# Scan and top-1 expert kernel: traced landing times in the build-time scheduler, six chunks turned by TensorE, new ranks

## The chip, the core and the metric

The kernel runs on one core of one Trainium2 chip. The metric is the device time of one execution in microseconds (us); a figure for a kernel is the median of several executions. A profiled execution gives the trace, from which all the rows below are read. TensorE is PE in the profile, VectorE DVE, ScalarE ACT, GpSimd POOL and SyncE SP.

## What is computed

Two steps, one behind the other, over 4 sequences of 5056 tokens with 256 channels each. The first is a gated recurrence along the sequence; the second sends each token to one of 8 experts (256 to 1024 to 256).

```python
sig = 1.0 / (1.0 + np.exp(-f_logit))
f = lower_bound + (1.0 - lower_bound) * sig
h[t] = f[t] * h[t - 1] + (1 - f[t]) * x[t]          # per sequence and channel, h starts at 0

logits = h @ w_gate
e_idx = np.argmax(logits, axis=1)
gate_w = softmax(logits)[e_idx]
eom = sigmoid(h @ w_output_gate)
out[token] = gate_w * eom[e_idx] * (relu(h @ w1[e_idx]) @ w2[e_idx])
```

## The kernel before

**Chunks.** The 20224 tokens are worked on in 40 chunks of up to 512. For each chunk SP's queue loads two halves of 512 KB each, `f` and `x` (L493, into one of four buffers, the tiles `fx`). ScalarE takes a tanh (L554) and the forget gate (L562), VectorE a product (L557) and the scan (L568), one of each for both halves of the channels. ScalarE squares (L577), TensorE sums the squares (L582), and from that VectorE takes a power of two for each channel (the small steps L341 to L351) by which the rows are split into a high part (ScalarE, L596) and a rest (VectorE, L599). TensorE then multiplies both by the gates (L629, L636). A chain of small steps on VectorE finds the expert of each token (L664 to L685) and its place in the expert's list (L692 to L738, `dst`); L748 to L756 write the two factors beside the row.

**Turning and scattering.** The rows leave the chunk token by token, so they are turned first. For chunks from `FLIP` on, SP's queue does it with four transposing DMAs a chunk (`turn`, L606, 128 KB each). For chunks ahead of `FLIP`, TensorE transposes (`flip`, L616, two times 8 matmuls of 128x128) and ScalarE copies the result to `rows` (`settle`, L622, two a chunk). GpSimd then scatters the rows to `scr` in device memory, 128 tokens an instruction (`send`, L760, four a chunk). Chunks 0, 6 and 8 are worked on together with the next one; so chunks 0 and 1 share one chain of small steps, and 2 has its own. Ahead of the first scatter two DMAs write the pad rows of `scr` (L451).

**Weights.** Each expert's weights come in four loads of 512 KB (L961, tiles `w1s`, `w2s` and a `spare`). TensorE sums their squares (L1002), VectorE finds a norm (L1011 and small steps, up to `cinv`, L1018), ScalarE writes the high part (L1025) and VectorE the rest (L1029).

**Expert tiles.** A tile is up to 256 tokens of one expert. SP's queue gathers its rows from `scr`, transposed (`xq`, L1068), with the factors (`mt`, L1071); a list (`firsts`, L876, read on SP by L1064) says where they lie. The first tile of each expert is made by `first` (L1174 to L1243): four quarters of 12 matmuls up (L1190 to L1192), a high part (ScalarE, L1197), a rest (VectorE, L1201, `el`) and 12 matmuls down (L1214 to L1216). The first tile of expert 0 needs chunks 0 to 2 scattered. The tiles after those are the same with their weights copied to a buffer (L1095 on VectorE; up L1120 to L1122, high part L1129, rest L1137, down L1168 to L1170). The result is scaled on ScalarE (L1254) and scattered to the output by GpSimd (L1258).

**What sets the order.** A scheduler runs when the kernel is built. Every operation is an `Op` with an engine, an estimated cost, the operations that it needs, and, for a DMA, `ship`, its share of the DMA rings. `Clock.start` estimates when an operation could start; `Clock.drive` takes, on each engine, those that could start within 0.2 us of the earliest, and of them the one with the lowest number in `RANK`; `Clock.run` emits it and books its end. So the tables of numbers and the estimates set the order in which each engine's instructions stand. Loads of chunks and of weights are held behind the VectorE instruction that was emitted last.

Of the kernel before, what the change touches and what calls it, by code (L numbers as in the profile page):

```python
# [43 lines left out]
AHEAD = 10  # L44
EIGHT = 6
RANK = {
    "setup": (-1.79,),
    "pad": (111.84,),
    "steady": (1083.0, -252.28, -120.37, -372.54, 593.86, 324.22, 400.43, 793.4,),
    "tiles": (686.39, 292.5, 1654.95, 552.0, 347.5, 547.63, 517.82,),  # L50
    "first": (-278.52, 1564.55,),
    "plan": (417.78, 434.95,),
    "load": (-665.55, -89.61, 940.76, 394.74, -259.08, 259.99, 78.44, 300.77, 561.91, 301.96,),
# [7 lines left out]
    "gram": (93.14, -61.7, 1485.49, -210.01, 145.26, 421.5, 1186.44, -100.15,),  # L61
    "norm": (436.94, -280.81, 498.9, -288.2, 719.44, -78.73, 333.59, 983.81,),
    "w0": (1378.71, -304.56, 873.38, -252.27, 459.78, -57.06, 397.41, 465.44,),
    "w1": (1021.41, 4435.66, 1660.07, -256.31, 878.52, -188.54, 427.66, 629.66,),
}
# [5 lines left out]
VEC, ACT, TEN, GPS, SYN = "VATGS"  # L71
# [3 lines left out]
BACKLOG = 2.0  # L75
FLIP = 3
QUICK = 10
# [10 lines left out]
class Op:  # L88


    def __init__(self, eng, cost, fn, needs=(), key=None, stage=0, ring=None, ship=0.0, bulk=False, lazy=False, group=None,
                 shift=0.0, lag=0.0, margin=0.0, late=False, gap=False):
        self.eng, self.cost, self.fn, self.needs, self.key = eng, cost, fn, tuple(needs), key
        self.group, self.shift = group, shift
        self.stage, self.ring, self.ship, self.bulk, self.lazy = stage, ring, ship, bulk, lazy
        self.lag, self.margin, self.late, self.gap = lag, margin, late, gap
        self.done = False
# [22 lines left out]
class Clock:  # L120
# [56 lines left out]
    def run(self, o, t):  # L177
# [15 lines left out]
        if o.ship:  # L193
            self.bus = max(self.bus, t + (1.2 if o.eng == GPS else min(o.cost, 1.0))) + o.ship
            end = self.bus + SHIP + (1.2 if o.bulk else 0.2)
            if o.eng == SYN:
                self.out.append(end)
        elif o.eng == TEN:
            end += 0.16
            if self.on and o.lag:  # L200
                end += o.lag
                self.aside.add(o.key)
# [33 lines left out]
def tile_scan_moe(  # L236
# [258 lines left out]
    def chunk_load(c):  # L495
        past = 0 if c < 4 else 4 if c < 6 else 2
        held = [("turned", c - past), (c - past, "pr"), (c - past + 1, "scan0"), (c - past + 1, "scan1")] if past else []
        group, shift = (("load", c), 0.0) if c < AHEAD else (("steady", 6), 2 * TILE * (c - AHEAD))
        return [
            Op(SYN, 0.5, lambda i=i: load_part(c, i), held, ("fx"[i], c), ship=1.34, bulk=True, group=group, shift=shift)  # L500
            for i in range(2)
        ]

    def bunch(i):
# [289 lines left out]
        for c in cs:  # L794
            for k in range(KD):
                op(7, ACT, 0.72, lambda c=c, k=k: high(c, k), ["sa", (c, "sq0"), (c, "sq1")], (c, f"h{k}"), c)
            for k in range(KD):
                op(8, VEC, 0.76, lambda c=c, k=k: rest(c, k), [(c, f"h{k}")], (c, f"l{k}"), c)
                if c >= FLIP:
                    op(8, SYN, 1.28, lambda c=c, k=k: turn(c, 0, k), [(c, f"h{k}"), *gone(c)], (c, f"turn0{k}"), c, ship=0.78)  # L800
            if c < FLIP:
# [6 lines left out]
            else:  # L808
                for k in range(KD):
                    turn1.append((10, SYN, 1.28, lambda c=c, k=k: turn(c, 1, k), [(c, f"l{k}"), *gone(c), *(["oh"] if c >= AHEAD else [])],  # L810
                                  ("turned", c) if k == KD - 1 else (c, f"turn1{k}"), c))
                    if c < AHEAD:
                        op(*turn1[-1], ship=0.78)
        prs = [(c, "pr") for c in cs]
# [9 lines left out]
        if c1 >= AHEAD:  # L824
            for x in turn1:
                op(*x, ship=0.78, late=True)
        op(14, TEN, 0.16 * (nb + 1) / 5, all_before, ["oh"], "pk", lag=1.4)
# [12 lines left out]
        for c in cs:  # L840
            for b in range(size[c] // P):
# [3 lines left out]
                   (c, "sent") if b == size[c] // P - 1 else None, c, ship=0.55, late=AHEAD <= c < NCH - 1 and b > 0,  # L845
                   gap=AHEAD <= c < NCH - 1)
        if c1 == NCH - 1:
# [110 lines left out]
    def expert_load(e):  # L958

        return [  # L960
            Op(SYN, 0.5, lambda h=h, z=z: nc.sync.dma_start(out=crude(e, h, z), in_=wT[SLOTS[e]][:, h * WH + z * QH : h * WH + (z + 1) * QH]),  # L961
               [(0, "sent")] if e == E - 1 else [], ("w", e, h, z), ship=1.32, bulk=True, group=("wl", e))
            for h in range(2) for z in range(2)
# [210 lines left out]
    def first(e):  # L1174
# [55 lines left out]
        need = [(c, "sent") for c in range(EARLY[e])] + [("tab", groups.index(EARLY[e])), ("free",)]  # L1230
        op(4 * e, SYN, 2.3, fetch, need, key("x"), ring=("xq", 3, key("up", 3)), ship=1.8)
        for q in range(4):
# [308 lines left out]
```

## Time and profile before

| | us |
|---|---|
| median of 3 runs | 955.34 |
| lowest, highest | 954.16, 959.31 |
| profiled execution | 959.21 |
| its span in the trace | 957.5 |
| TensorE busy | 903.9 (94%) |
| VectorE busy | 739.0 (77%) |
| ScalarE busy | 541.2 (57%) |
| GpSimd busy | 354.1 (37%) |

The span runs from the first to the last instruction in the trace; the execution's own time is 1.7 us longer. A busy share is a mean over the whole span, and this kernel has two parts: a front in which chunks and weights are made ready and no expert tile can run, and a long stretch in which TensorE has tiles throughout. So the profile has to be read by stretches. The mean granted clock of TensorE over the span was 0.98 of full speed.

### The profile page before, as it was taken

How to read it: one execution, taken by the hardware profiler on the slowest of the kernel's cores; microseconds unless marked ns; L12 is line 12 of the kernel's file. 1: busy time of each engine (PE TensorE's matmuls, PEld its weight loads, DVE VectorE, ACT ScalarE, POOL GpSimd, SP SyncE). 2: the span in 40 equal slices, each digit the busy share in tenths (PEclk: the TensorE clock that was granted, in tenths of full speed). 3: DMA queues.
4: the chain of work that ended last, by engine and by line, in shares of the span. 5: the costliest groups of instructions: out<-in, count | busy, mean ns of one | idle time of the engine just before them, and what ended most of it. 6: DMA issues, size and time to landing. Idle time of an engine off the chain costs nothing.

```text
span 957.5 us, 26500 instructions
## 1 busy us (share of the span) xinstructions
PE 903.9 (94%) x9504; PEld 812.7 (85%) x9504; DVE 739.0 (77%) x2048; ACT 541.2 (57%) x1184; POOL 354.1 (37%) x382
## 2 busy tenths in 40 slices
PE   3569999999999999999999999999999999999997
PEld 3458888888888888888888888888888888899996
DVE  6879889788877887878878789787888778445554
ACT  6959586656465655657556576464655543223332
POOL 1533163443534344343443435435344342212122
PEclk9669999999999999999999999999999999999999
DMA  9988974765656767666766658645666443112110
GB/s 334 350 187 225 290 202 95 201 158 135 152 148 180 148 157 153 145 175 155 169 146 139 184 146 169 151 131 149 166 166 155 109 114 92 51 34 61 42 44 26
DMA packets 229739, 144.44 MB, mean 151 GB/s; under 512 B 193611, under 2 KB 195404, under 8 KB 229600
## 3 DMA queue, kind: packets, MB, share of 16 engines
q1 hardware_dynamic: 214016, 99.90, 44.5%
q0 software_dynamic: 15296, 42.73, 13.6%
q8 instruction: 79, 1.29, 0.6%
q14 instruction: 60, 0.49, 0.2%
q10 hardware_dynamic: 288, 0.02, 0.0%
HBM read 58.38 MB, written 44.37 MB: 107 GB/s over the span
## 4 chain that ended last, share of the span: by engine, by line
PE 66%; DMA 10%; DVE 9%; issue 8%; ACT 4%; POOL 1%; SPq 0%; POOLq 0%; DVEq 0%; ACTq 0%
PE ph L1120 11%; PE py L1168 11%; PE ph L1121 10%; PE ph L1122 10%; PE py L1169 10%; PE py L1170 10%; DMA out_dram<-yo,mt 3%; DVE fx L568 3%; DMA fx<-in_xT_dram 3%; POOL out_dram L1258 1%; DMA fx<-in_fT_dram 1%; DVE fx L557 1%; DMA mt<-scr 1%; PE rw L636 1%; DVE el L1201 1%
## 5 line engine op out<-in xcount | busy, mean ns | idle before, releaser
L1122 PE MATMUL ph<-xq,w 128*128 128x256 f16 (+2 forms) x1312 | 326.6, 259 | 0.0
L1120 PE MATMUL ph<-xq,w 128*128 128x256 f16 (+2 forms) x1312 | 326.1, 259 | 0.3 <-DMA xq<-scr 0.3
L1121 PE MATMUL ph<-xq,w 128*128 128x256 f16 (+2 forms) x1312 | 326.4, 259 | 0.0
L1129 ACT ACTIVATE hh<-ph 128x512 f16<-128x512 f32 (+1 forms) x312 | 173.1, 555 | 246.0 <-PE ph L1122 218.6
L1168 PE MATMUL py<-w2s,hh 128*128 x1136 | 309.0, 272 | 2.5 <-issue 1.9
L1170 PE MATMUL py<-w2s,hl 128*128 x1136 | 309.4, 272 | 0.0
L1169 PE MATMUL py<-w2s,hh 128*128 x1136 | 309.2, 272 | 0.0
L1258 POOL DMA_INDIRECT out_dram<-yo,mt x146 | 157.3, 1078 | 291.5 <-ACT yo L1254 239.3
L760 POOL DMA_INDIRECT scr<-rows,dst x158 | 165.3, 1046 | 261.1 <-DVE hl L1137 34.5
L1137 DVE SCALAR_TENSOR_TENSOR hl<-ph,hh 128x512 f16<-128x512 f32 (+1 forms) x312 | 197.5, 638 | 68.1 <-ACT hh L1129 62.9
L1095 DVE COPY w<-w1s 128x2048 f16 x164 | 118.3, 721 | 43.4 <-PE ph L1122 36.7
L1120 PEld LDWEIGHTS <-w 128*128 128x128 f16 x1312 | 127.6, 98 | 12.0 <-issue 0.6
L1122 PEld LDWEIGHTS <-w 128*128 128x128 f16 x1312 | 127.4, 97 | 11.8
L1121 PEld LDWEIGHTS <-w 128*128 128x128 f16 x1312 | 127.4, 97 | 10.1
L1168 PEld LDWEIGHTS <-hh 128*128 128x128 f16 x1136 | 110.7, 97 | 15.2 <-issue 3.7
L1170 PEld LDWEIGHTS <-hl 128*128 128x128 f16 x1136 | 110.6, 97 | 13.1
L1169 PEld LDWEIGHTS <-hh 128*128 128x128 f16 x1136 | 110.6, 97 | 10.2
L568 DVE TENSOR_TENSOR_SCAN fx<-fx,fx 128x512 f32<-128x512 f32 (+4 forms) x78 | 95.0, 1238 | 3.4 <-ACT fx L562 3.3
L562 ACT ACTIVATE fx<-fx,fb,fa 128x512 f32<-128x512 f32 (+1 forms) x80 | 61.6, 801 | 33.8 <-DVE fx L557 33.8
L1254 ACT ACTIVATE yo<-py,fac 128x256 f32<-128x256 f32 (+1 forms) x146 | 61.9, 469 | 28.3 <-PE py L1170 24.1
L599 DVE SCALAR_TENSOR_TENSOR fx<-fx,sa 128x512 f16<-128x512 f32 (+1 forms) x80 | 55.9, 740 | 10.4 <-ACT fx L596 10.3
L636 PEld LDWEIGHTS <-fx 128*128 128x128 f16 x632 | 52.9, 97 | 7.4 <-DVE fx L599 1.5
(177 smaller groups left out, 1196.6 us busy)
## 6 DMA issues: line engine op xcount, KB each, us to landing
fx<-in_fT_dram SPq DMA_DIRECT2D x39, 512.0 KB
fx<-in_xT_dram SPq DMA_DIRECT2D x39, 512.0 KB
w1s<-in_wT_dram SPq DMA_DIRECT2D x14, 512.0 KB
w2s<-in_wT_dram SPq DMA_DIRECT2D x14, 512.0 KB
scr<-rows,dst POOLq DMA_INDIRECT x158
rows<-fx SPq DMA_TRANSPOSE x148
out_dram<-yo,mt POOLq DMA_INDIRECT x146
spare<-in_wT_dram SPq DMA_DIRECT2D x4, 512.0 KB
```

The lines of the kernel that those rows point to most:

```text
L568: nc.vector.tensor_tensor_scan(out=xt(c)[:, k, a:z], data0=ft(c)[:, k, a:z], data1=xt(c)[:, k, a:z], initial=init, op0=ALU.mult, op1=ALU.add,)
L760: ins = nc.gpsimd.indirect_dma_start(out=scr[:, :], out_offset=IOA(ap=H["dst"][:, j : j + 1], axis=0), in_=lines[:, j, :], in_offset=None)
L1095: nc.vector.tensor_copy(out=w, in_=w1f[:, ds(T["ev"] * (2 * WH) + h * 2 * QH, 2 * QH)])
L1120: nc.tensor.matmul(out=o, lhsT=w[:, f, k, 0, :], rhs=T["xh"][:, k, 0:n], start=first, stop=False)
L1121: nc.tensor.matmul(out=o, lhsT=w[:, f, k, 0, :], rhs=T["xl"][:, k, 0:n], start=False, stop=False)
L1122: nc.tensor.matmul(out=o, lhsT=w[:, f, k, 1, :], rhs=T["xh"][:, k, 0:n], start=False, stop=last)
L1129: nc.scalar.activation(hh[:, :, 0:n], ph[:, :, 0:n], AF.Relu)
L1137: nc.vector.scalar_tensor_tensor(out=hl[:, :, 0:n], in0=ph[:, :, 0:n], scalar=0.0, in1=hh[:, :, 0:n], op0=ALU.max, op1=ALU.subtract)
L1168: nc.tensor.matmul(out=o, lhsT=hh[:, i, c], rhs=wh, start=first, stop=False, skip_group_check=True)
L1169: nc.tensor.matmul(out=o, lhsT=hh[:, i, c], rhs=wl, start=False, stop=False, skip_group_check=True)
L1170: nc.tensor.matmul(out=o, lhsT=hl[:, i, c], rhs=wh, start=False, stop=last, skip_group_check=True)
L1258: ins = nc.gpsimd.indirect_dma_start(out=out[:, :], out_offset=IOA(ap=T["mt"][0 : T["p"], b, 2:4].bitcast(I32), axis=0), in_=T["yo"][0 : T ...
```

## The change

Four things change. `FLIP` goes from 3 to 6: the rows of chunks 3, 4 and 5 are turned by TensorE and copied by ScalarE, where SP's queue turned them with twelve transposing DMAs. The estimates of the scheduler change: a chunk's load, a weight's load and a transposing DMA take larger shares of the rings, and an operation can have a landing time (`land`), 2.0 for scatters and for the gathers of the first tiles, which is added to its end. All the ranks of the front are new numbers (two rows of the table stand below), and the rows "steady" and "tiles" of the table stay. Nothing else is changed; TensorE has 48 transposes more and ScalarE six copies more.

```diff
 RANK = {
...
     "steady": (1083.0, -252.28, -120.37, -372.54, 593.86, 324.22, 400.43, 793.4,),
     "tiles": (686.39, 292.5, 1654.95, 552.0, 347.5, 547.63, 517.82,),
-    "first": (-278.52, 1564.55,),
+    "first": (283.02, 978.35,),
...
-FLIP = 3
+FLIP = 6
...
-        self.lag, self.margin, self.late, self.gap = lag, margin, late, gap
+        self.lag, self.margin, self.late, self.gap, self.land = lag, margin, late, gap, land
...
-            end = self.bus + SHIP + (1.2 if o.bulk else 0.2)
+            end = self.bus + SHIP + (1.2 if o.bulk else 0.2) + o.land
...
-            Op(SYN, 0.5, lambda i=i: load_part(c, i), held, ("fx"[i], c), ship=1.34, bulk=True, group=group, shift=shift)
+            Op(SYN, 0.5, lambda i=i: load_part(c, i), held, ("fx"[i], c), ship=1.47, bulk=True, group=group, shift=shift)
...
-                    op(8, SYN, 1.28, lambda c=c, k=k: turn(c, 0, k), [(c, f"h{k}"), *gone(c)], (c, f"turn0{k}"), c, ship=0.78)
+                    op(8, SYN, 1.28, lambda c=c, k=k: turn(c, 0, k), [(c, f"h{k}"), *gone(c)], (c, f"turn0{k}"), c, ship=1.01)
...
-                   gap=AHEAD <= c < NCH - 1)
+                   gap=AHEAD <= c < NCH - 1, land=2.0)
...
-               [(0, "sent")] if e == E - 1 else [], ("w", e, h, z), ship=1.32, bulk=True, group=("wl", e))
+               [(0, "sent")] if e == E - 1 else [], ("w", e, h, z), ship=1.45, bulk=True, group=("wl", e))
...
-        op(4 * e, SYN, 2.3, fetch, need, key("x"), ring=("xq", 3, key("up", 3)), ship=1.8)
+        op(4 * e, SYN, 2.3, fetch, need, key("x"), ring=("xq", 3, key("up", 3)), ship=1.8, land=2.0)
```

How the instructions move is seen in each engine's order. In it `fx_135` is the buffer of chunk 0 and again of chunk 4, `fx_136` of 1 and 5, `fx_133` of 2, and `fx_134` of 3.

On SP, the loads behind chunk 0's stand like this before:

```order
L493 DMA fx_136<-in_fT_dram 128x2x512
L451 DMA scr<-padt 128x544 x2
L493 DMA fx_136<-in_xT_dram 128x2x512
L493 DMA fx_134<-in_fT_dram 128x2x512
L493 DMA fx_134<-in_xT_dram 128x2x512
L961 DMA w1s<-in_wT_dram 128x1024 x2
L961 DMA w2s<-in_wT_dram 128x1024 x2
L493 DMA fx_133<-in_fT_dram 128x2x512
L493 DMA fx_133<-in_xT_dram 128x2x512
```

And on SP in the changed kernel:

```order
L451 DMA scr<-padt 128x544 x2
L493 DMA fx_136<-in_fT_dram 128x2x512
L493 DMA fx_136<-in_xT_dram 128x2x512
L493 DMA fx_133<-in_fT_dram 128x2x512
L493 DMA fx_133<-in_xT_dram 128x2x512
L961 DMA w1s<-in_wT_dram 128x1024 x2
L961 DMA w2s<-in_wT_dram 128x1024 x2
L961 DMA w1s<-in_wT_dram 128x1024 x2
L961 DMA w2s<-in_wT_dram 128x1024 x2
L493 DMA fx_134<-in_fT_dram 128x2x512
```

Chunks 2 and 3 changed places, four weight loads instead of two stand ahead of the later of them, and the pad went ahead of chunk 1.

On SP, the end of the front, up to the first gather (`xq`), stands like this before:

```order
L961 DMA w2s<-in_wT_dram 128x1024 x2
L961 DMA w1s<-in_wT_dram 128x1024 x2
L961 DMA w2s<-in_wT_dram 128x1024 x2
L606 DMA_TRANSPOSE rows<-fx_134 128x4x128 x4
L961 DMA w1s<-in_wT_dram 128x1024
L1064 TENSOR_LOAD firsts
L1064 ISA x2
L1068 ISA
L1068 DMA_TRANSPOSE xq<-scr 128x4x256
```

And in the changed kernel:

```order
L961 DMA w1s<-in_wT_dram 128x1024 x2
L961 DMA w2s<-in_wT_dram 128x1024 x2
L961 DMA w1s<-in_wT_dram 128x1024 x2
L961 DMA w2s<-in_wT_dram 128x1024 x2
L1064 TENSOR_LOAD firsts
L1064 ISA x2
L1068 ISA
L1068 DMA_TRANSPOSE xq<-scr 128x4x256
```

The transposes of chunk 3 and the weight load that stood between them and the gather are gone from there.

On VectorE, around the first rest of an expert tile (`el`; `pf_n`, `done` are steps of the list `firsts`, `w1s` and `w2s` rests of weights, `es`, `eg` and `fc` factors of a chunk), before:

```order
L867 TENSOR_SCALAR pf_n<-pf_n 128x5
L869 TENSOR_SCALAR done_142<-pf_n 128x5
L871 TENSOR_TENSOR pf_n<-bfree,pf_n 128x5
L1029 SCALAR_TENSOR_TENSOR w1s<-w1s,wi 128x8x128 x2
L1201 SCALAR_TENSOR_TENSOR el<-ph,eh 128x512
L748 SCALAR_TENSOR_TENSOR fc<-es,eg 128x4
L1201 SCALAR_TENSOR_TENSOR el<-ph,eh 128x512 x2
```

And in the changed kernel (`cinv` ends the norms of a group of experts; `xr`, `xi` are powers of two of a chunk):

```order
L1018 SCALAR_TENSOR_TENSOR cinv<-wr 128x2
L568 SCALAR_TENSOR_TENSOR fx_136<-fx_136,fx_135 128x512
L1029 SCALAR_TENSOR_TENSOR w2s<-w2s,wi 128x4x256
L1201 SCALAR_TENSOR_TENSOR el<-ph,eh 128x512 x2
L341 TENSOR_SCALAR xr<-rw_119 128x1
L345 TENSOR_SCALAR xr<-xr 128x1
L348 TENSOR_SCALAR xi<-xr 128x1
L1201 SCALAR_TENSOR_TENSOR el<-ph,eh 128x512
L1029 SCALAR_TENSOR_TENSOR w2s<-w2s,wi 128x4x256
```

The first tile's rests now stand behind a norm and a scan of chunk 5, and of the rests of weights that stood ahead of them, some follow between them.

## Rows read from the trace of the kernel before

**Rows 1.** Head of the profile's page.

```profile
span 957.5 us, 26500 instructions
```

**Rows 2.** Stretches: start:end, length, busy (instructions) of PE, PEld, DVE, ACT, POOL, PEclk, DMA share, GB/s.

```profile
59.30:65.30 6.00, 5.92 (x28) 4.24 (x29) 0.96 (x3) 2.32 (x4) 0.96 (x1) 0.50 0.92 164
59.40:72.00 12.60, 12.60 (x97) 10.30 (x98) 6.39 (x14) 6.55 (x10) 3.49 (x4) 0.76 0.83 192
72.00:92.00 20.00, 19.62 (x211) 17.59 (x209) 19.85 (x30) 19.10 (x36) 4.14 (x5) 1.00 0.79 210
92.00:100.00 8.00, 5.23 (x61) 4.53 (x59) 4.62 (x12) 5.11 (x8) 3.27 (x3) 1.00 1.00 339
100.00:167.50 67.50, 64.91 (x718) 58.27 (x715) 60.52 (x144) 48.33 (x96) 26.58 (x26) 1.00 0.72 186
```

**Rows 3.** PE in time: start, duration (us), engine, line, operation, names, [idle before <-releaser].

```profile
21.70 1.50 PE L616 MATMUL rt<-ident,fx 128*128 128x128 f16 x24
...
59.38 0.37 PE L1190 MATMUL ph<-xq,w1s 128*128 128x256 f16 x1 [3.81 <-DMA xq<-scr]
59.54 0.42 PE L1191 MATMUL ph<-xq,w1s 128*128 128x256 f16 x1
...
65.30 0.31 PE L1191 MATMUL ph<-xq,w1s 128*128 128x256 f16 x1
```

**Rows 4.** PE in time, steady tiles: the first matmuls of two quarters.

```profile
170.37 0.27 PE L1120 MATMUL ph<-xq,w 128*128 128x256 f16 x1 [0.31 <-DMA xq<-scr]
...
172.99 0.27 PE L1120 MATMUL ph<-xq,w 128*128 128x256 f16 x1
```

**Rows 5.** DVE in time: first note of chunk 2, first L1137.

```profile
47.28 0.23 DVE L756 TENSOR_SCALAR rows<-fc,xr 128x4 f32<-128x4 f32 x1 [0.39 <-DMA scr<-rows,dst]
...
167.45 0.68 DVE L1137 SCALAR_TENSOR_TENSOR hl<-ph,hh 128x512 f16<-128x512 f32 x1
```

**Rows 6.** DVE in time, 14 to 27 us: chunks 2 and 3.

```profile
14.99 1.27 DVE L557 SCALAR_TENSOR_TENSOR fx<-fx 128x512 f32<-128x512 f32 x2
...
18.41 2.74 DVE L599 SCALAR_TENSOR_TENSOR fx<-fx,sa 128x512 f16<-128x512 f32 x4 [1.70 <-ACT fx L596]
...
22.54 1.29 DVE L557 SCALAR_TENSOR_TENSOR fx<-fx 128x512 f32<-128x512 f32 x2 [1.06 <-DMA fx<-in_xT_dram]
...
26.50 0.20 DVE L664 TENSOR_REDUCE mx<-rw 128x8 f32<-128x64 f32 x1
```

**Rows 7.** POOL in time: the first, eighth and twelfth scatter.

```profile
32.23 1.25 POOL L760 DMA_INDIRECT scr<-rows,dst  x1 [26.77 <-ACT sa L589]
...
42.77 0.99 POOL L760 DMA_INDIRECT scr<-rows,dst  x1 [0.55 <-DVE firsts L876]
...
48.20 0.99 POOL L760 DMA_INDIRECT scr<-rows,dst  x1 [0.17 <-issue]
```

**Rows 8.** SP's queue in time: four transposes, the first gather.

```profile
47.30 5.25 SPq L606 DMA_TRANSPOSE rows<-fx  x4
...
54.32 1.25 SPq L1068 DMA_TRANSPOSE xq<-scr  x1
```

**Rows 9.** Groups by form, 0 to 60 us: names, shapes, xcount | busy us, mean ns | idle before.

```profile
L568 DVE TENSOR_TENSOR_SCAN fx<-fx,fx 128x512 f32<-128x512 f32 x8 | 9.9, 1273 | 0.6 <-ACT fx L562 0.6
...
L622 ACT ACTIVATE rows<-rt 128x1024 f16<-128x1024 f16 x6 | 6.0, 1008 | 0.3 <-DMA scr<-rows,dst 0.3
...
L1029 DVE SCALAR_TENSOR_TENSOR w1s<-w1s,wi 128x1024 f16<-128x1024 f32 x4 | 5.0, 1275 | 0.0
```

**Rows 10.** PE's waits, 59 to 168 us: engine line waited for: total us, times, longest.

```profile
PE pg L1002 <- DMA w2s<-in_wT_dram: 1.7, 1, 1.7
```

**Rows 11.** A stretch, columns as in rows 2; eight transposes on SP's queue.

```profile
153.80:166.50 12.70, 12.38 (x158) 11.18 (x156) 10.71 (x33) 6.57 (x17) 3.35 (x4) 1.00 0.51 105
```

**Rows 12.** DVE, POOL, SP's queue: from a chunk's targets to the gather.

```profile
251.24 0.19 DVE L738 TENSOR_REDUCE dst<-pos 128x4 int32<-128x32 f32 x1
...
263.27 0.97 POOL L760 DMA_INDIRECT scr<-rows,dst  x1 [0.30 <-issue]
...
270.35 1.30 SPq L1068 DMA_TRANSPOSE xq<-scr  x1
```

More of the change, by code (lines that the diff above doesn't have):

```diff
@@ L46 @@
 RANK = {
-    "setup": (-1.79,),
-    "pad": (111.84,),
+    "setup": (670.53,),
+    "pad": (782.01,),
     "steady": (1083.0, -252.28, -120.37, -372.54, 593.86, 324.22, 400.43, 793.4,),
     "tiles": (686.39, 292.5, 1654.95, 552.0, 347.5, 547.63, 517.82,),
-    "first": (-278.52, 1564.55,),
-    "plan": (417.78, 434.95,),
-    "load": (-665.55, -89.61, 940.76, 394.74, -259.08, 259.99, 78.44, 300.77, 561.91, 301.96,),
[7 rows of a table removed]
[L61 to L64, printed above, removed]
+    "first": (283.02, 978.35,),
+    "plan": (-266.62, 920.62,),
+    "load": (-346.35, 45.43, 315.58, 908.38, -280.69, 191.96, -319.25, 345.91, 886.01, -510.61,),
[7 rows of a table added]
+    "gram": (775.91, 298.97, 505.72, -1084.79, 953.13, 398.97, -12.15, 47.17,),
+    "norm": (418.26, 433.3, 509.44, -501.15, 783.85, 932.45, 927.56, -208.38,),
+    "w0": (615.31, 5658.49, 1077.74, 3059.66, 473.88, -186.71, -133.62, 420.85,),
+    "w1": (2160.23, -434.07, 283.12, 911.0, 1031.83, 738.97, -132.99, 1950.72,),
 }
@@ L91, in __init__ @@
     def __init__(self, eng, cost, fn, needs=(), key=None, stage=0, ring=None, ship=0.0, bulk=False, lazy=False, group=None,
-                 shift=0.0, lag=0.0, margin=0.0, late=False, gap=False):
+                 shift=0.0, lag=0.0, margin=0.0, late=False, gap=False, land=0.0):
         self.eng, self.cost, self.fn, self.needs, self.key = eng, cost, fn, tuple(needs), key
@@ L812, in bunch @@
                     if c < AHEAD:
-                        op(*turn1[-1], ship=0.78)
+                        op(*turn1[-1], ship=1.01)
         prs = [(c, "pr") for c in cs]
@@ L825, in bunch @@
             for x in turn1:
-                op(*x, ship=0.78, late=True)
+                op(*x, ship=1.01, late=True)
         op(14, TEN, 0.16 * (nb + 1) / 5, all_before, ["oh"], "pk", lag=1.4)
```

14 rows, old and new, of the table RANK are left out of this document.

## The prediction

> **What bounds the kernel now.** I read the page first, then TensorE by stretches, then back from its first long work to what held it. The profiled execution took 959.21 us, span 957.5 [rows 1]. TensorE is busy for all but a few per cent of it, so time can be won only where it is idle or slow. By stretches, behind its first long work 72 to 92 us lacks 0.38 us, 92 to 100 lacks 2.77, 100 to 167.5 lacks 2.59 [rows 2]; the rest lies ahead of that work. The first expert tile starts at 59.38 us, after 3.81 us of waiting for its gathered rows, and runs 5.92 us, 0.42 us a matmul, at a granted clock of 0.50 (the 1.2 GHz level), until they shorten at 65.30 [rows 2, 3]. A quarter of an expert tile is 12 matmuls up and 12 down, and the next one starts 2.62 us behind it [rows 4]; on VectorE it shows as one L1201 or L1137. The first L1137, the 33rd quarter, is at 167.45 [rows 5]. From there TensorE waits for nothing of size. I count in the new program's order that up to this 33rd quarter VectorE, ScalarE and TensorE have done the same expert tiles, the same weights and the same chunks in both kernels; so the result is the move of that one moment. In the kernel before, the 108.07 us between the two moments are 5.74 us of gaps [rows 2], 2.96 us lost to the low clock (half of 5.92), and 99.4 us of work.
>
> **The change part by part.**
>
> *Loads.* Chunk 2 is loaded in the place chunk 3 had. Its input landed at 22.54 and VectorE waited 1.06 us for it; chunk 3's, two rows of the queue earlier, cost it no wait at 14.99 [rows 6]. The scan of chunk 2 then fits behind that, into the 1.7 us in which VectorE waited for ScalarE's first high part, and its second half behind the four rests that end at 21.15, so at 22.3 [rows 6]. The maxima of chunks 0 and 1 started at 26.50, behind chunk 2's scan and 24 transposes on TensorE [rows 6]; now they need only the 48 gate matmuls behind the rests, so about 22.7, and their last step comes near 26. I lay chunk 2 behind it in the same way, with ScalarE's copies and weights between, and get its list of first tiles (the row `firsts`) at 33. The pad goes ahead of chunk 1's load: two issues of under 0.5 us each, and nothing if the ring is full; I take 0 and keep 1 us in the range.
>
> *Scatters.* Twelve stood between 32.23 and 48.20 [rows 7], 1.45 us apart. From 27 on they end near 44.7, since the last four wait for ScalarE's copies of chunk 2 at about 40. A scatter lands some 3.5 us after its issue ends (the eighth ended at 43.76 and released VectorE at 47.28 by its landing [rows 5, 7]), so at 48.2.
>
> *First gather.* Before, it stood behind four transposes and a weight load and was issued at 54.32; its data came 3.81 us after the issue had ended [rows 3, 8]. Now neither is ahead of it: 48.2 + 1.25 + 3.8 = 53.3. The data stop being what the first tile waits for.
>
> *What is late next.* In the new order the first tile stands behind the norms of four experts, the gates of chunk 4 and its 16 transposes. VectorE does two of the weight rests ahead of it, not six, two row rests fewer, one scan and one product more, 13 small steps fewer: by durations 4 x 1.28 + 2 x 0.69 - 1.27 - 0.64 = 4.6 us [rows 6, 9], and some 1.6 us of small steps (0.2 us where each waits for the last [rows 6], half of it where two chains alternate). If VectorE idled as before, the first tile would start at 59.4 - 6.2 = 53.2. It cannot quite: from 33 on I count 51 large and small steps of 20.9 us up to the last norm, and waits of 1.5 us for ScalarE's squares and high parts and 1.6 us for TensorE's products of weights at the low clock. That gives 57.4. Bounds: 54 (no waits) and 60 (ScalarE's six more copies, 6 x 1.01 us [rows 9], pass on a half). ScalarE is nearly full from 26 to 55, so I take 57.4: **2.0 us earlier**.
>
> *Clock.* The clock rose only behind 5.92 us without a pause, and what stands far ahead of the first tile is as sparse as before. But gates, 16 transposes and 32 products now stand close ahead of it, where before the last 3.81 us were a wait [rows 3]. The loss is between 0 and 2.96 us; I take 2.0: **1.0 us less**.
>
> *48 transposes more.* 32 fall into TensorE's idle time ahead of the first tile and cost nothing there. 16, of chunk 5, stand behind it: 24 ran from 21.70 in 1.50 us [rows 3], so **1.0 us more**.
>
> *Gaps up to the 33rd quarter.* The 2.77 us between 92 and 100 were waits for halves of weights, the longest 1.7 [rows 2, 10]. In the new order that expert's four loads stand four gathers ahead of their use and not two, and 12 transposes are gone from the rings. Eight transposes in 12.7 us took a DMA share of 0.51 [rows 11], 0.8 us of all rings each, so 9.6 us are freed. I take these waits away and add 1.0 us of new ones, because VectorE has 101 us of work for the 106 us that are left and less slack than before: **1.7 us less**. Bounds 1 and 8 us of gaps.
>
> Here a page speaks against the change: the Trainium skill, Advanced Engine Details and Errata, X-Bar Transpose (TRN2), says that transpose DMAs are as fast as regular ones. The 0.8 us for the 128 KB of one here are twice what plain loads take at a full share (339 GB/s [rows 2], 0.39 us), so the trace disagrees. By the rule some 4 us of rings would be freed, half of the weights' wait could stay, and the sum would be 1.4 us worse.
>
> *Planner numbers* (`ship`, `land`) and ranks only move instructions. Behind the 33rd quarter the chunks now come one per eight quarters throughout, where before they crept ahead. I count no time for it (the rival below prices it). ScalarE's copies behind the first tile lie beside 1.3 us matmul groups.
>
> **The sum.** 57.4 + 99.4 + 1.0 + 2.0 + 4.0 = 163.8 against 167.45: 3.7 us, so 955.5 for the profiled execution. That one is 3.9 us above the median of 955.34 of the three runs (954.16 to 959.31), so the forecast for the median is **951.7 us**, 0.4% less. A difference of 0.5%, 4.8 us, is about the least that a measurement can tell here.
>
> **The rivals.**
>
> *A. Front and clock both come off (faster).* The first tile starts at 56, TensorE is at 2.4 GHz by then, and only 2.5 us of gaps stay: 56 + 100.4 + 2.5 = 158.9, 8.5 us less, 946.8. For it: VectorE's own floor is no later, and the data are there by 53. Against: VectorE and TensorE would both have to run with almost no waits for 100 us. Part of the way, any gain of over 4.8 us, is enough to count.
>
> *B. VectorE sets the end (no change).* Its work up to the 33rd quarter is the same total in both, some 145 us; if it idles 22 us as before, the early start is given back between 60 and 160 and the time is 954 to 956. For it: it is at 19.85 of 20 us from 72 to 92 already [rows 2]. Against: 6.2 of its idle microseconds lay between 59.4 and 72 [rows 2], where it waited for the first tile at the low clock; the new order has weights for that place.
>
> *C. Gathers come late throughout (slower).* Tiles come in groups of four per two chunks. From the targets of the second chunk to the first use the new order has 12 quarters, 31.4 us, for all 14 of them from tile 7 on; the kernel before had 11 to 13 at first and 24 at the end. The chain inside: targets at 251.24, last scatter ends at 264.24, gather issued at 270.35 [rows 12], data some 5 us later: 24 us. Two of the last scatters, not one, now stand behind the output writes, about 3 us more. It turns against the change if the chain passes 31.4 us; at 33 us it costs 14 x 1.6 = 22 us, less 3.7: 973. Against: tiles 7 to 14 ran with that lead before, and TensorE waited 0.31 us once for a gather [rows 4].
>
> **How the numbers follow.** Forecast 0.40; A 0.38; B 0.10; C 0.07; smaller losses (a late load in the ramp, ScalarE's copies in full) 0.05. Faster by over 0.5%: 0.38. Within: forecast and B, 0.50. Slower: 0.12. The likeliest case's own range is 949.5 to 954.5. The range for 8 in 10 goes from A with its bounds, 946.0, to B with a late ramp, 957.5; C stays outside.
>
> **What the profile would show.** Right: chunk 2's product on VectorE near 15, first scatter near 27, first gather issued near 48 to 50 with no transpose ahead of it, first tile at 56 to 59 and released by a norm or a product rather than by gathered rows; no wait for halves of weights over 1 us; first L1137 at 161 to 166. Wrong: the first tile still released by gathered rows; a new gap over 3 us between 60 and 160; TensorE waiting for gathers behind 170; or the first L1137 moved and the end not.

## The result and the profile after

The changed kernel takes 948.03 us (median of 5 runs, 946.05 to 949.22) against 956.43 us before (5 runs, 954.16 to 959.31): a ratio of 0.9908, with a 95% interval of 0.9881 to 0.9934. The whole interval lies below 0.995, so it is faster by more than the 0.5% that the prediction took as the least that can be told. The forecast was 951.7 us, in a range of 946.0 to 957.5. The profiled executions are 13.2 us apart (959.21 and 946.05), the medians 8.4, because the one of before lies 2.8 us above its median and the other 2.0 us below. So what is read off these two traces overstates the change by some 5 us, and where I can I use the second pair of traces (e5, e6) as well.

The page's head and TensorE's busy time:

```profile
span 944.3 us, 26535 instructions
...
PE 902.7 (96%) x9552; PEld 814.6 (86%) x9552; DVE 746.3 (79%) x2048; ACT 546.7 (58%) x1190; POOL 363.6 (38%) x382
```

The front in time. First TensorE (start, duration, line, operation, idle before), then its weight loads, then VectorE, GpSimd's scatters of chunk 0 and chunk 2's last, and the first gather on SP's queue:

```profile
53.48 1.87 PE L616 MATMUL rt<-ident,fx 128*128 128x128 f16 x16
55.14 1.91 PE L1002 MATMUL pg<-w2s 128*128 128x128 bf16 x16
...
57.67 0.16 PE L1014 MATMUL rw<-l,ones 128*128 128x4 bf16 x1 [0.50 <-DVE pos L712]
57.69 0.27 PE L1190 MATMUL ph<-xq,w1s 128*128 128x256 f16 x1
```

```profile
57.67 0.10 PEld L1190 LDWEIGHTS <-w1s 128*128 128x128 f16 x1 [0.56 <-DMA xq<-scr]
```

```profile
14.35 1.27 DVE L557 SCALAR_TENSOR_TENSOR fx<-fx 128x512 f32<-128x512 f32 x2
...
23.02 0.23 DVE L664 TENSOR_REDUCE mx<-rw 128x8 f32<-128x64 f32 x1 [1.33 <-PE rw L636]
...
161.75 0.69 DVE L1137 SCALAR_TENSOR_TENSOR hl<-ph,hh 128x512 f16<-128x512 f32 x1
```

```profile
27.68 1.44 POOL L760 DMA_INDIRECT scr<-rows,dst  x1 [22.13 <-DVE fx L599]
...
45.88 1.49 POOL L760 DMA_INDIRECT scr<-rows,dst  x1 [0.30 <-issue]
```

```profile
51.95 1.41 SPq L1068 DMA_TRANSPOSE xq<-scr  x1
```

The front went as laid out: chunk 2's products where chunk 3's were, the maxima at 23.02 and not 26.50 [rows 6], the first scatter at 27.68 and not 32.23 [rows 7]. The first tile starts at 57.69 us, 1.69 earlier [rows 3], behind transposes and products with one wait of 0.50 us just ahead of it, and its matmuls take 0.27 us from the first one, where before 28 of them ran at the low level. The norm's product starts at 57.67, and at the same moment ends the first weight load's wait of 0.56 us for the gathered rows.

The stretches up to the 33rd quarter, which is at 161.75 instead of 167.45 [rows 5]; columns as in rows 2:

```profile
57.69:72.00 14.31, 13.31 (x170) 12.22 (x170) 13.89 (x46) 11.87 (x19) 5.60 (x5) 1.00 0.93 248
72.00:92.00 20.00, 20.00 (x201) 18.11 (x199) 19.46 (x29) 18.81 (x33) 8.29 (x8) 1.00 1.06 302
92.00:100.00 8.00, 7.17 (x85) 6.46 (x84) 8.00 (x10) 6.03 (x12) 0.00 (x0) 1.00 1.11 274
100.00:161.75 61.75, 60.22 (x657) 54.11 (x655) 54.13 (x128) 46.89 (x88) 26.08 (x23) 1.00 0.67 163
...
161.75:944.30 782.55, 775.20 (x8086) 699.02 (x8083) 605.41 (x1700) 416.02 (x950) 298.78 (x302) 1.00 0.56 132
```

The gaps here are 1.00, 0, 0.83 and 1.53 us, 3.36 in sum, against 5.74. The last line runs to the end; its counterpart in the kernel before is this one, with one stretch of it:

```profile
250.00:400.00 150.00, 147.45 (x1470) 131.72 (x1468) 122.49 (x361) 87.30 (x200) 61.16 (x63) 1.00 0.62 150
...
167.45:957.50 790.05, 777.81 (x8096) 700.48 (x8094) 598.56 (x1699) 417.62 (x953) 295.98 (x304) 1.00 0.54 132
```

TensorE idles 12.24 us there before and 7.35 after, and both have some 7.5 us of that behind 800 us, at the kernel's end. Between the 33rd quarter and 800 us it is 4.6 us before and under 0.1 after. This is what I had not counted. The waits are short and alike; one of them in the kernel before, on TensorE in time:

```profile
359.06 0.16 PE L582 MATMUL rw<-hss,na 128*128 128x1 bf16 x1 [0.98 <-ACT fx L577]
359.86 0.27 PE L1168 MATMUL py<-w2s,hh 128*128 x1 [0.64 <-issue]
```

A chunk's sums of squares stand on TensorE before ScalarE has the squares, and the expert matmuls behind them wait too, though for these the profile names no releaser (`issue`). This one belongs to the chunk whose targets stand at quarter 109 in the order of before, the third of a quick run: 90, 96, 101, 109, at distances of 6, 5 and 8. In the changed order the distances are 11 and 5 in turn throughout.

The 13.2 us of the two traces are then: 1.69 at the first tile; 4.01 up to the 33rd quarter (2.96 low clock and 2.38 gaps, less 1.3 because at that moment the changed kernel has also done the next quarter's products, 37 recorded matmuls of the steady kind against 26); and 7.50 behind (4.89 of gaps, that same 1.3, and 1.3 which no listed wait shows).

### The profile page after: what moved, and what is told of

The parts are those of the page before. It is cut to its first block, busy times and chain, and to the rows that moved or that the text cites. A ratio compares the mean times of both kernels' runs of the same rounds, so it can differ in the third digit from the quotient of the medians.

```text
span 944.3 us, 26535 instructions
## 1 busy us (share of the span) xinstructions
PE 902.7 (96%) x9552; PEld 814.6 (86%) x9552; DVE 746.3 (79%) x2048; ACT 546.7 (58%) x1190; POOL 363.6 (38%) x382
## 4 chain that ended last, share of the span: by engine, by line
PE 76%; issue 7%; DVE 6%; DMA 5%; ACT 4%; POOL 1%; POOLq 0%; ACTq 0%; DVEq 0%
PE ph L1120 12%; PE py L1168 12%; PE ph L1122 12%; PE ph L1121 12%; PE py L1170 11%; PE py L1169 11%; DMA out_dram<-yo,mt 3%; POOL out_dram L1258 1%; DVE fx L568 1%; PE rw L636 1%; DVE w2s L1029 1%; DVE el L1201 1%; DVE w1s L1029 1%; PE pg L1002 1%; DMA w2s<-in_wT_dram 1%
## 5 line engine op out<-in xcount | busy, mean ns | idle before, releaser
L760 POOL DMA_INDIRECT scr<-rows,dst x158 | 170.2, 1077 | 235.0 <-DVE w L1095 64.7
L1137 DVE SCALAR_TENSOR_TENSOR hl<-ph,hh 128x512 f16<-128x512 f32 (+1 forms) x312 | 198.7, 641 | 73.7 <-ACT hh L1129 69.1
L1095 DVE COPY w<-w1s 128x2048 f16 x164 | 116.4, 710 | 31.0 <-PE ph L1122 30.7
```

Source lines behind the costliest of these rows:

```text
L760: ins = nc.gpsimd.indirect_dma_start(out=scr[:, :], out_offset=IOA(ap=H["dst"][:, j : j + 1], axis=0), in_=lines[:, j, :], in_offset=None)
L1095: nc.vector.tensor_copy(out=w, in_=w1f[:, ds(T["ev"] * (2 * WH) + h * 2 * QH, 2 * QH)])
L1137: nc.vector.scalar_tensor_tensor(out=hl[:, :, 0:n], in0=ph[:, :, 0:n], scalar=0.0, in1=hh[:, :, 0:n], op0=ALU.max, op1=ALU.subtract)
```

## The experiments

They ran on three chips, e1 to e4, e5 to e8 and e9 to e12 together, and each ratio is to the kernel before on the same chip (973.96, 958.39 and 976.62 us). The kernel before is 16 to 18 us slower on the first and the third of them, so times are compared within a group only.

**e1, the new estimates for chunks from 10 on alone.** The front stays as before.

```diff
-            Op(SYN, 0.5, lambda i=i: load_part(c, i), held, ("fx"[i], c), ship=1.34, bulk=True, group=group, shift=shift)
+            Op(SYN, 0.5, lambda i=i: load_part(c, i), held, ("fx"[i], c), ship=1.47 if c >= AHEAD else 1.34, bulk=True, group=group, shift=shift)
...
-                op(*x, ship=0.78, late=True)
+                op(*x, ship=1.01 if c >= AHEAD else 0.78, late=True)
...
-                   gap=AHEAD <= c < NCH - 1)
+                   gap=AHEAD <= c < NCH - 1, land=2.0 if c >= AHEAD else 0.0)
```

> The kernel before with the new ship and land estimates for chunks from 10 on alone: its front is the same word for word up to the targets of chunk 9, and behind it the chunks come one per eight quarters, the last at quarter 273 and not 261, as in the changed kernel. Theory P (the even pace of the chunks is worth time by itself): TensorE's 4.9 us of idle behind the 33rd quarter (12.2 us in the trace before, 7.3 us in the changed one, of which 7 us are the tail in both) go away; 3 to 5 us less than before, the first expert tile at 59.4 us as before, no listed wait of TensorE behind 170 us over 0.5 us. Rival F (all of the gain comes from the front, and the waits behind 170 us were an accident of that one execution): within 1.5 us of before.

Measured: 969.06 us, ratio 0.9955 (0.9937 to 0.9973). Between 250 and 800 us TensorE idles 0.02 us. One new wait stands in the trace:

```profile
247.77 0.28 PE L1120 MATMUL ph<-xq,w 128*128 128x256 f16 x1 [4.74 <-DMA xq<-scr]
```

So the pace is worth time by itself (theory P), even with one gather 4.74 us late: a piece of the prediction's rival C, in one place.

**e2, the changed kernel with the old pace behind its front.** The reverse edit: the new estimates only where `c < AHEAD`.

> The changed kernel with the old ship and land estimates for chunks from 10 on alone: its front is that of the changed kernel, and behind it the chunks creep ahead as in the kernel before (last targets at quarter 261). Theory P: the front alone is worth about 4 us against before, and the waits of TensorE behind 170 us come back, some 4 us in sum; so 952 us, 3 to 5 us above the changed kernel. Rival F: within 1.5 us of the changed kernel (948), 8 us below before.

Measured: 968.04 us, ratio 0.9947 (0.9925 to 0.9968). TensorE idles 5.5 us between 250 and 800 us, mostly at such sums of squares. The front alone gives about half of the 0.9 to 1.0% that the changed kernel gives on other chips, as P has it. But the trace does not show this gain in the front. The first tile starts at 66.68 us and the 33rd quarter is at 174.37, where e1, with the old front on the same chip, has 60.59 and 166.54. VectorE comes late to the maxima and the places of chunk 2, from which the first tile's list is made:

```profile
34.67 0.19 DVE L664 TENSOR_REDUCE mx<-rw 128x4 f32<-128x32 f32 x1 [3.02 <-remote]
...
40.41 0.19 DVE L712 TENSOR_TENSOR pos<-rw,cnt 128x32 f32<-128x32 f32 x1 [4.20 <-remote]
```

In the changed kernel's trace the first of these waits is 0.16 us and the second is none. Here TensorE's products that the two steps read end 2.4 and 4.1 us before the steps start; what held them stays open. The 33rd quarter is 8 us later than in e4 as well, which has the old front and the old pace; most of that is made up right behind it, since up to the 40th it takes 15.2 us here and 21.7 in e4. From there to the 100th quarter e2 and e4 stay within 1.5 us of each other. So where the front's 0.5% comes from on this chip isn't settled.

**e3, the changed order, chunks 3 to 5 turned by SP.**

```diff
         def flip(c, i):
+            if c >= 3:
+                for k in range(KD):
+                    made = turn(c, i, k)
+                return made
...
         def settle(c, j):
+            if c >= 3:
+                return None
```

> The changed kernel's order, but the rows of chunks 3 to 5 are turned by SP's transposing DMAs, which stand where TensorE's transposes stood; ScalarE's copies of these chunks are left out. Theory T (turning by TensorE is what counts): four transposes stand ahead of the first gather again (5 us of SP's queue), 9.6 us of the rings are taken back, and the first tile finds TensorE idle ahead of it; first tile at 60 to 63 us, low clock for some microseconds, waits for halves of weights over 2 us behind it; 4 to 9 us above the changed kernel. Rival O (the order of chunks, norms and weights is what counts, the turning is hidden either way): within 2 us of the changed kernel.

Measured: 969.09 us, ratio 0.9948 (0.9923 to 0.9974). From the first tile to the 33rd quarter, first of this kernel, then of e2, which has the same front turned by TensorE:

```profile
65.23:182.28 117.05, 106.73 (x1100) 93.64 (x1099) 96.20 (x209) 82.29 (x147) 38.95 (x37) 0.95 0.81 196
```

```profile
66.68:174.37 107.69, 103.76 (x1099) 92.05 (x1100) 95.82 (x208) 83.32 (x149) 37.47 (x36) 0.97 0.78 206
```

And what TensorE waited for in that stretch of e3 (total us, times, longest):

```profile
PE pg L1008 <- DMA w1s<-in_wT_dram: 4.8, 2, 3.6
```

The first tile is 1.5 us earlier than in e2, but the 33rd quarter is 7.9 us later, and the wait for halves of weights is back. In the new order the turning by TensorE counts (theory T). The two times are level because e3 has the even pace: it takes 785.4 us from the 33rd quarter to the end, e2 794.5. The distance of e3 to the changed kernel itself wasn't taken on that chip.

**e4, TensorE kept busy ahead of the first tile, in the kernel before.**

```diff
+        def fill():
+            spin = pp.tile([P, 2, 2 * D], F16, tag="h", name="spin", bufs=4)
+            for _ in range(28):
+                nc.tensor.transpose(out=spin[:, 0, 0:P], in_=ident, identity=ident)
...
         def all_before():
             for s in range(nb + 1):
                 aside(before, s)
+            if c1 == 4:
+                aside(fill)
```

> The kernel before with 28 transposes of a constant on TensorE, whose result nobody reads, in the 3.8 us in which TensorE waits for the first gather. Theory C (the low clock of the first tile comes from that wait, and its price is real): the first tile runs at 0.27 us a matmul from its start at 59.4 or within 1 us of it, the 5.9 us at a granted clock of 0.50 shrink to under 1.5, and the end comes 2 to 3 us earlier. Rival W (the first tile's haste is given back at the weights that TensorE waits for at 92 to 100 us, whose loads the rings set): the clock is up, the wait for halves of weights at 92 to 100 us grows from 2.8 to over 5 us, and the time stays within 1 us of before. Rival N: the clock does not follow what TensorE did just ahead; rows of 0.42 us up to 65 us as before, no change.

Measured: 975.15 us, ratio 1.0018 (0.9994 to 1.0041). TensorE in time:

```profile
57.83 3.15 PE L702 MATMUL spin<-ident 128*128 128x128 f16 x28
61.19 0.37 PE L1199 MATMUL ph<-xq,w1s 128*128 128x256 f16 x1 [0.21 <-PE spin L702]
...
61.70 0.27 PE L1199 MATMUL ph<-xq,w1s 128*128 128x256 f16 x1
```

With the 28 transposes just ahead, the clock is up half a microsecond into the first tile; in e1, which has the same front without them, 15 matmuls run at the low level, up to 63.7 us. So theory C is right on the clock. But the end does not move, and the interval excludes C's 2 to 3 us. On this chip there was less to win: 15 matmuls at 0.21 us apart and not 0.11, some 1.6 us. The stretch to the 33rd quarter, here and in e1:

```profile
61.19:166.36 105.17, 99.83 (x1077) 88.90 (x1078) 91.88 (x197) 78.77 (x146) 37.39 (x35) 1.00 0.84 205
```

```profile
60.59:166.54 105.95, 101.31 (x1077) 89.61 (x1078) 92.33 (x198) 78.75 (x146) 39.27 (x35) 0.98 0.78 204
```

TensorE is busy 1.5 us less and idle 0.7 us more, and the tile started 0.6 us later, so the 33rd quarter is 0.2 us earlier. The gain is given back, but not where rival W put it: the waits for halves of weights did not grow (1.4 us in sum, 1.8 in e1).

**e5 and e6, the two kernels once more,** for a second pair of traces.

> The kernel before, once more, for a second trace of it. If the waits of TensorE behind the 33rd quarter belong to its order (theory P), over 3 us of idle stand again between that quarter and 800 us, beside chunks that creep ahead; if they were an accident of one execution, under 1 us. The time is that of before within 0.2%.

> The changed kernel, once more, beside the others of this call. 0.7 to 1.2% below before; under 1.5 us of idle of TensorE between the 33rd quarter and 800 us; first expert tile 1 to 3 us ahead of that of before, at the full clock.

Measured: 958.51 us, ratio 1.0002 (0.9986 to 1.0018), and 948.54 us, ratio 0.9901 (0.9883 to 0.9918). The same stretch in e5 and e6:

```profile
250.00:400.00 150.00, 147.33 (x1468) 131.67 (x1467) 121.96 (x356) 88.76 (x203) 62.44 (x64) 1.00 0.63 153
```

```profile
250.00:400.00 150.00, 150.00 (x1497) 134.52 (x1495) 123.04 (x328) 89.09 (x200) 62.03 (x62) 1.00 0.62 148
```

The waits belong to the order: 5.5 us against 0.02 between the 33rd quarter and 800 us, and the old order's stand at the same places as in the first trace (quarters 40, 89, 91, 104 and 148 in both). The first tile starts at 61.74 and 58.67, the 33rd quarter is at 169.14 and 162.78.

**e7, chunks 3 to 5 turned by TensorE in the old order.**

```diff
         def turn(c, i, k):
+            if 3 <= c < 6:
+                if k == KD - 1:
+                    flip(c, i)
+                    if i:
+                        for j in range(NB // 2):
+                            settle(c, j)
+                return None
```

> The kernel before in its own order, but the rows of chunks 3 to 5 are turned by TensorE and copied by ScalarE, at the places in the program where SP's transposing DMAs stood. Theory T (turning by TensorE is what gives the front's part of the gain): the first gather is issued some 4 us earlier, 9.6 us of rings come free, the first tile starts at 57 to 58.5 us; 2 to 5 us less than before. Rival O (the new order gives it): the flips and copies only get in the way of the products and high parts of the old order; within 1.5 us of before, or slower.

Measured: 958.31 us, ratio 1.0011 (0.9997 to 1.0024). The first tile starts 6.6 us earlier than in e5, and the 33rd quarter is at 167.77 against 169.14. TensorE in time, then ScalarE and GpSimd:

```profile
55.12 0.39 PE L1197 MATMUL ph<-xq,w1s 128*128 128x256 f16 x1
...
146.95 0.16 PE L582 MATMUL rw<-hss,na 128*128 128x1 bf16 x1 [3.44 <-ACT fx L577]
...
147.75 0.42 PE L1198 MATMUL ph<-xq,w1s 128*128 128x256 f16 x1
```

```profile
143.93 0.84 ACT L1261 ACTIVATE ey<-py,fac 128x256 f32<-128x256 f32 x2 [2.94 <-DMA out_dram<-ey,mt]
```

```profile
132.60 0.96 POOL L767 DMA_INDIRECT scr<-rows,dst  x1 [5.04 <-DMA rows<-fx]
...
138.71 1.43 POOL L1265 DMA_INDIRECT out_dram<-ey,mt  x1 [0.30 <-issue]
```

The stretches around it:

```profile
120.00:137.00 17.00, 17.00 (x159) 15.23 (x157) 15.10 (x21) 15.28 (x26) 9.86 (x10) 1.00 0.96 229
137.00:150.00 13.00, 9.12 (x76) 7.65 (x74) 10.45 (x20) 9.38 (x18) 6.31 (x6) 0.87 0.29 85
```

Read backwards: TensorE waits 3.44 us for a chunk's squares; on ScalarE these stand behind a tile's result, which waits 2.94 us for its one buffer `ey`; that buffer is held by the last output write, which on GpSimd stands behind scatters that waited 5.04 us for rows of a later chunk, turned on SP's queue. The first trace of before has that wait too (4.98 us), but there ScalarE comes to the result at 146.00, 5 us later than here, and finds `ey` free. Up to 137 us the rests of first tiles run 5 us ahead of the first trace of before (137.4 against 142.4 for the 25th); the last one is level (162.1 and 162.2). Behind the wait the clock is at the 1.2 GHz level again, 0.42 us a matmul. So rival O: in the old order the wait and the low clock behind it take what the front won.

**e8, e7 with the even pace of e1.**

> As the one before, with the even pace of the chunks from 10 on beside it: so both parts without the new ranks. If the parts add and the ranks of the front give nothing by themselves, it stands within 0.3% of the changed kernel, some 0.8% below before. If the new ranks carry the front, it shows the pace alone, 0.4 to 0.5% below before.

Measured: 959.67 us, ratio 1.0019 (1.0003 to 1.0036): neither of the two. The waits behind 250 us are gone (0 us idle up to 400), and the late gather of e1 is back:

```profile
240.26 0.39 PE L1127 MATMUL ph<-xq,w 128*128 128x256 f16 x1 [5.16 <-DMA xq<-scr]
```

It costs what the pace wins on this chip, 5.2 us and some matmuls at the low level behind it. So turning and pace without the new ranks give nothing here, where the changed kernel gives 1.0%; how much of that the late gather alone takes isn't shown.

**e9, one number: the turn's share for chunks from 10 on.**

```diff
-                    op(8, SYN, 1.28, lambda c=c, k=k: turn(c, 0, k), [(c, f"h{k}"), *gone(c)], (c, f"turn0{k}"), c, ship=0.78)
+                    op(8, SYN, 1.28, lambda c=c, k=k: turn(c, 0, k), [(c, f"h{k}"), *gone(c)], (c, f"turn0{k}"), c, ship=1.01 if c >= AHEAD else 0.78)
...
-                op(*x, ship=0.78, late=True)
+                op(*x, ship=1.01 if c >= AHEAD else 0.78, late=True)
```

> The kernel before with one estimate changed: a transposing DMA's share of the rings is 1.01 and not 0.78 for chunks from 10 on. In its order this alone gives the even pace of the chunks (the targets of chunks 10 to 39 stand at the same quarters as in the changed kernel, the last at 273), and chunk 9 stays where it was, at quarter 50, where the run with all the new estimates had it at 53 and one gather 4.7 us late. Theory P: the waits of TensorE behind 170 us (4.6 and 5.5 us in two traces of before) go away without a late gather; 3 to 5 us less than before. Rival L (the even pace makes a gather late wherever the front is that of before): one wait of 4 to 5 us for gathered rows near 240 us, no gain.

Measured: 964.89 us, ratio 0.9869 (0.9837 to 0.9901), more than P's 3 to 5 us: 12 us. Its six runs lie within 2.4 us, the 23 of before on this chip within 10.9. Its stretches, and then those of e12, which has the old pace, on the same chip:

```profile
250.00:400.00 150.00, 150.00 (x1499) 134.53 (x1497) 118.70 (x351) 82.98 (x187) 62.01 (x64) 1.00 0.62 152
400.00:600.00 200.00, 200.00 (x2008) 179.38 (x2006) 160.47 (x445) 116.66 (x265) 81.63 (x83) 1.00 0.63 148
```

```profile
250.00:400.00 150.00, 145.88 (x1442) 129.74 (x1441) 119.20 (x352) 85.66 (x196) 62.75 (x65) 1.00 0.66 158
400.00:600.00 200.00, 195.84 (x1958) 174.00 (x1956) 160.12 (x465) 115.79 (x265) 79.86 (x84) 0.99 0.64 148
```

No gather is late and no wait is left in these 350 us, where the old pace idles 8.3 us in e12 and 5.0 in e10 below, which has e9's front and is the closer comparison. From the 33rd quarter to the end e9 idles 12.6 us and e10 20.0. So some 7.5 of the 12 us are seen as waits; the profiled run of e10 was its quickest, and where the others lose more isn't shown.

**e10 and e11, VectorE spared eight rests,** in the kernel before and in the changed one.

```diff
         def lo(h, z):
             (t, r), (l, _) = parts(e, h, 0, z), parts(e, h, 1, z)
+            if e >= 4 and h:
+                nc.vector.memset(l, 0.0)
+                return
```

> The kernel before with less work for VectorE between the first expert tile and the 33rd quarter: eight rests of second weights (experts 4 to 7, 1.28 us each) are left out, and VectorE writes zeros in their place, in the same place of its order. The result lacks these low parts. Theory V (VectorE sets the 33rd quarter, so that an earlier first tile and a faster clock are given back): that quarter comes earlier by at least half of what VectorE is spared, 2 to 6 us, though the first tile starts as before, and so does the end. Rival S (what sets it is the weights' arrival and ScalarE's copies, VectorE only waits for them): VectorE's idle time grows by what it is spared, the quarter moves by under 1 us.

> The same eight rests left out in the changed kernel. Theory V: VectorE is busy for 92% of the time between the first tile and the 33rd quarter there, so it sets this stretch all the more; 2 to 6 us less than the changed kernel. Rival S: under 1 us less, since TensorE already runs with 3.5 us of gaps in that stretch and no gap can be won but these.

Measured: 978.66 us, ratio 1.0014 (0.9986 to 1.0042), and 962.67 us, ratio 0.9846 (0.9814 to 0.9878). In e10 one memset on VectorE, and the stretch from the first tile to the 33rd quarter:

```profile
107.72 0.48 DVE L1030 MEMSET w2s<- 128x512 uint32 x1
```

```profile
59.16:167.18 108.02, 100.97 (x1077) 89.76 (x1078) 87.69 (x199) 78.88 (x146) 38.51 (x35) 0.99 0.79 201
```

VectorE was spared 8 times 0.8 us, 6.4 in sum. The same stretch of e9, with the same front and all its rests, is 109.48 us long (61.76 to 171.24); TensorE's busy time in it, the low clock included, is 2.9 us longer than here and its idle time 1.5 us shorter. So sparing VectorE won TensorE no time, and the interval excludes a gain of over 0.14%, or 1.4 us. Theory V falls for the old order. For the new one, e11's time can't be told from what e9 and e12 give together (0.983), since the changed kernel itself did not run on that chip. Its trace speaks against V as well: the first tile starts at 63.26 and the 33rd quarter is at 172.28, against 63.19 and 171.84 in e12, which has the same front with all its rests.

**e12, e2 once more.**

> The changed kernel's front with the pace of before behind it, once more, beside the others of this call. If front and pace add: 0.4 to 0.6% below before, with waits of TensorE at the same places as in before behind 170 us (a chunk's products of squares, then the next matmul) of 4 to 5 us in sum, and the 33rd quarter where the changed kernel has it, 161 to 163 us.

Measured: 972.82 us, ratio 0.9958 (0.9932 to 0.9983). The front alone again gives some 0.4%, with the old waits behind it (10 us of idle between 250 and 800 us, two lines of it above). The 33rd quarter is at 171.84, not at the 161 to 163 expected, and no earlier than with the old front on that chip (171.24 in e9, 167.18 in e10). The two `remote` waits shown under e2 stand here too, with 2.25 and 2.83 us.

## Why the prediction was right, and where it was not

The sign and the range hold, and so does the mechanism of the front in the two pairs of traces (before and after, e5 and e6); the size does not. The forecast was 3.7 us, measured are 8.4 and 9.9.

*Loads, scatters, first tile.* Right: 57.69 (58.67 in e6) against 57.4, though the terms given for that (33, 20.9, 1.5 and 1.6) add up to 57.0, and on the other two chips the new front has it at 63 to 67 (e2, e11, e12). The step on the gather was wrong: I had it issued at 48.2 and its data at 53.3, it was issued at 51.95. Its twelve scatters took 19.7 us, to 47.37 and not 44.7, and it could go only behind the landing of the last, 4.6 us on and not 3.5. The data are no longer early; they come with the norm's product, so the sign "released by a norm or a product rather than by gathered rows" was half met.

*Clock.* Mis-sized: I took 2.0 us of loss, it was 0. Transposes and products stand close ahead of the tile, as the sum had it, with one wait of 0.50 us, and the granted clock is 1.00 from its start. But e4 says that this term is no term by itself: in the old order it moves nothing.

*Gaps.* 4.0 forecast, 3.36 measured; the wait for halves of weights is at most 0.8 us. e3 puts the transposes back on the rings, and 4.8 us of it return. The Trainium skill, Advanced Engine Details and Errata, X-Bar Transpose (TRN2), has transposing DMAs as fast as regular ones. The stretch of [rows 11] disagrees: it moved 105 GB/s at a share of 0.51, some 206 at a full one, where plain loads moved 339. But three output writes ran in it too; by bytes the eight transposes are 1.05 of its 1.33 MB, so one took some 0.6 us of the rings and not the prediction's 0.8.

*16 transposes.* They are there, with 1.1 us. TensorE's busy time up to the 33rd quarter, less the low clock, is 99.4 us before and 100.7 after. That is less than these and the next quarter's products together; what became shorter isn't shown.

*The sum of the front* was 3.7 us at the 33rd quarter; that moment came 5.7 us earlier (161.75 and not 163.8), and 6.4 in the second pair of traces, so 2.1 us more than the sum had, by the clock (2.0) and the gaps (0.6) less 0.6 of a later start and more work. The front with the old pace gives 0.53% and 0.42% (e2, e12), 4 to 5 us. That these are near 3.7 bears out nothing, since on their chips the 33rd quarter did not come earlier. And the terms do not add: an earlier tile (e7), a faster clock (e4) and less work for VectorE (e10), each alone in the old order, gave nothing; e7 shows how, with ScalarE's one buffer. In the new order they come together, and e3 shows that at least the turning is needed. What else in the new order lets it keep the gain isn't settled.

*Planner numbers.* The step that failed: "I count no time for it". The even pace of chunks behind the 33rd quarter is a good part of the change. In the first pair of traces it is 4.6 of the 13.2 us. On the chip of e1 and e2 it gives 0.45%, with a late gather, beside the front's 0.53%, and on that of e9 and e12 1.31%, without one, beside 0.42%. I had read that "TensorE waits for nothing of size" there; single waits are under 1 us, but they come to 4.6 us. The sum of a stretch would have told.

*Rivals.* A was nearest in time (946.8 against 948.03), with its full clock, but by luck: it had 8.5 us from the front, which gave 5.7, and its first tile at 56 did not come. B's shape, an early start given back between 60 and 160, is what e7 does in the old order, and e4 with its faster clock, but not because VectorE is full (e10). Its work from the first tile to the 33rd quarter, put at 101 us, is 95.5. C happened at one gather, 4.7 to 5.2 us (e1, e8), where the new pace follows the old front with chunk 9 three quarters later; e9 and the changed kernel have chunk 9 in its old place and no such wait.

## What to carry to other kernels

Before calling a long stretch full, add up its idle time from the busy row of the stretch; many waits under 1 us hide from a list of the longest. A relief at the start of a stretch is worth only what the next in-order queue lets through, so try it alone before adding it to a sum. And where a planner spaces periodic work, an irregular spacing can cost the bound engine a short wait at the crowded places, the same ones in both traces of before (see e5): one estimate that evens it out (e9) can be worth more than a reworked front.

## What the runs showed of the hardware

The chips differ: the same kernel before takes 956 to 958 us on two occasions and 974 and 977 on the others. On the slower ones TensorE has waits at the start of the steady part for which the profile shows no releaser, as in e9:

```profile
181.35 0.37 PE L1169 MATMUL py<-w2s,hh 128*128 x1 [1.73 <-issue]
...
182.78 0.37 PE L1122 MATMUL ph<-xq,w 128*128 128x256 f16 x1 [0.42 <-issue]
```

The traces of before and after have none at that place. These waits differ with the front, too: between the 33rd quarter and 220 us TensorE idles 5.1 to 6.4 us with the old front on the slower chips (e1, e4, e9, e10) and 1.8 to 3.7 with the new one (e2, e11, e12), against 1.3 and 0.1 in before and after. Two more waits without a named cause, `remote` on VectorE, make the new front late on these chips (e2, e12). So a front that is earlier on one chip need not be on another.

The old pace idles 5.5 to 11.1 us between 250 and 800 us on the slower chips (e2, e4, e10, e12) where it idles 3.4 and 3.8 in before and e5. On either slower chip one trace has about twice the idle time of the other, so a gain from taking short waits away can differ by a factor of two from one trace to the next.
